# Three PSUM pairs and a bank for the second half of an attention phase: row maxima reduced two at a time

## The chip, the cores and the metric

The kernel runs on one core of one Trainium2 chip. The metric is device time in microseconds of one execution; the time given is the median of three runs. The work is spread over the core's engines: PE (matrix products into PSUM), DVE (VectorE, here above all the row maxima), ACT (ScalarE, here above all the exponentials), POOL, and SP, which issues most DMAs. [...]

## The reference, cut to what matters

```python
h = _layernorm(x) * (1 + ca) + sa
q, k, v = split(h @ wqkv)                 # 16 heads of 28, 2048 tokens
scores = einsum("bhqd,bhkd->bhqk", q, k) * 28 ** -0.5
p = softmax(scores)
o = einsum("bhqk,bhkd->bhqd", p, v)
x = x + ga * (o @ wo)
h = _layernorm(x) * (1 + cb) + sb
x = x + gb * (gelu(_layernorm(h) @ w1 + b1) @ w2 + b2)
```

All inputs are float32. The softmax subtracts the true maximum of each row, so each maximum has to be known before the exponentials of that row are taken.

## The kernel before, in words

There are three stages. First, LayerNorm and the projections. Second, attention. Third, the MLP. The change touches the second stage alone.

The 16 heads go in four groups of four (`g`), the 2048 queries in four tiles of 512 (`qt`); a **unit** `u` is one group and one query tile, 16 units in all. A unit has 16 **steps** (`kt`), each for 128 keys, so there are 256 steps, numbered `step = 16 u + kt`. Each of the four heads of a group takes 32 rows of the PE array, and a matmul of one head uses only those rows, so matmuls of different heads can run side by side.

One step issues, in this order:

- *First scores and second scores* (L1051). The scores of heads 0 and 1 of the group are six matmuls (three terms of a split product, two heads), into a tile `s` of two banks; those of heads 2 and 3 are six more into a second tile `s`. ACT takes the exponential of each tile whole (L1059, 128 x 1024).
- *Maxima* (L392, L397). The scores of later units are computed once more, roughly (one term instead of three), only for their row maxima: one matmul of 32 rows into a bank `mx`, and one VectorE reduction of 128 x 512 to 128 x 1. A unit needs 64 of them. `emit_max` puts three of them into one step and four into the next (`n_maxima`), between the score matmuls, and picks the heads whose rows the scores of that moment leave free.
- *Product with v* (L1015). Four matmuls that use the columns of the array, with the exponentials of the step before, into the bank `o`.

When the last maximum of a unit is in, `max_fin` gathers them, and two steps later their negatives go by DMA into the query operand of that unit.

From unit 12 on, each step with `kt` 8 to 11 also does a 128-token tile of the output projection (`t_wo`, whose matmuls are in `mm_acc`, L317): 9 matmuls in unit 12, 12 in units 13 to 15, of 128 rows and 128 columns, after the product with v, into a bank `mx`. ACT copies the result out (L812) and POOL adds it to `acc` (L813). Call these the **projection steps**; the other steps are plain. With `n_maxima`, a projection step has few maxima or none.

The PSUM banks of this stage: two pairs for `s`, three single banks `mx`, one `o`. When all maxima are done, `share(1, 3)` makes that three pairs `s`, one `mx`, one `o`. A tile waits for the engine that reads the one which had its banks before. A pool hands its tiles out in turn, and the order of instructions on each engine is the order of the code.

Of the kernel before, what the change touches and what calls it, by code (L numbers as in the profile page):

```python
# [22 lines left out]
D = 448  # L23
# [5 lines left out]
NB = S // 512  # L29
NG = H // 4  # L30
NKT = S // 128
# [10 lines left out]
def tile_adaln_block(ctx: ExitStack, tc: tile.TileContext, x, wqkv, wo, w1, b1, w2, b2, c, w_mod, out):  # L42
# [13 lines left out]
    def nm(t):  # L56
        uid[0] += 1
        return f"{t}_{uid[0]}"
# [253 lines left out]
    kh_sb = {}  # L312
    qh_sb = {}

    def mm_acc(p, terms):
        for i, (a, b) in enumerate(terms):
            pe.matmul(p, a, b, start=(i == 0), stop=(i == len(terms) - 1))  # L317

# [173 lines left out]
    def emit_max(n, half=None):  # L492
        for _ in range(n):
# [5 lines left out]
            max_one(g, qt, cch, i, j)  # L499
            count(g, qt, [cch])  # L500


    def emit_task(n, sixth, n_pairs):
        if not n:
# [254 lines left out]
    def unit_end_tasks(u, o_sb):  # L759
        g, qt = divmod(u, NB)  # L760
        st = {}
        staged = g < last_g(qt)
        parts = [g] if g > last_g(qt) else list(range(g + 1))

        def t_den():
            den = sbt("den", [128, 16], bufs=2)
            pool.dma_start(den, o_sb[DH:128:32, :].rearrange("j (q r) -> j q r", r=16))  # L767
            st["den"] = den

        def t_rec():  # L770
# [12 lines left out]
        def t_split2():  # L783
            on = st["on"]
            if u < NU - 1:
                hi = sbt("hi", [128, 512], F32R, bufs=3)
                lo = sbt("lo", [128, 512], F32R, bufs=3)
            else:
                hi = sb.tile([128, 512], F32R, tag=YTAGS[7], name="o_hi", bufs=1)
                lo = sbt("osb", [128, 512], F32R, bufs=2)  # L790
            dve.tensor_copy(hi, on)
            pool.tensor_tensor(out=lo, in0=on, in1=f(hi), op=ALU.subtract)
            st["hi"], st["lo"] = hi, lo
            if staged:
# [193 lines left out]
    pend = None  # L988
    o = None
    plain = [0]  # L990
    three = False


    def is_wo(s_):
        return s_ // NKT >= NU - NB and 8 <= s_ % NKT < 12


    def left_steps(s_):
        rest = range(s_, NKT * (NU - 1) - 6)
        n_wo = sum(is_wo(x) for x in rest)  # L1000
        return len(rest) - n_wo, sum(is_wo(x) and x % NKT > 8 for x in rest)


    def n_maxima(s_):
        n_plain, n_wo = left_steps(s_)
        over = len(mxq) - 7 * n_plain // 2
        if is_wo(s_):
            return max(0, -(-over // max(n_wo, 1))) if s_ % NKT > 8 else 0
        plain[0] += 1
        return 4 if plain[0] % 2 or (over > 3 * n_wo and over > 0) else 3  # L1010

    def av(u, kt, p, o):
        g = u // NB
# [10 lines left out]
        return slot(("c0", "c1", "d0")[p_no[0] % 3], [128, 4, 512], F32)  # L1024

    p_next = p_tile()
    done_max = set()
    for u in range(NU):
        g, qt = divmod(u, NB)
        for kt in range(NKT):  # L1030
            step = u * NKT + kt
            if kt == 1 and u + 1 < NU and u + 1 not in qst:
                load_q(u + 1)
            if kt == NKT - 6 and u + 1 < NU:
# [6 lines left out]
            n = n_maxima(step)  # L1041
            n0 = 1 if n == 3 and step % 4 == 3 else 2

            ks, qs = kst[(g, kt // 4)], qst[u]
            kc = slice((kt % 4) * 128, (kt % 4 + 1) * 128)
            for hf in range(2):
                s2 = ps_s2()
                for term, (kp, qp) in enumerate(((0, 0), (1, 0), (0, 1))):
                    for jj in range(2):
                        rows_ = slice(64 * hf + 32 * jj, 64 * hf + 32 * jj + 32)  # L1050
                        pe.matmul(s2[:, jj, :], ks[rows_, kp, kc], qs[rows_, qp, :], start=(term == 0), stop=(term == 2))  # L1051
                    if hf == 0 and term < min(n0, n):
                        emit_max(1, 1)
                    if hf == 1 and ((term == 0 and n - n0 > 0) or (term == 2 and n - n0 > 1)):
                        emit_max(1, 0)
                if hf == 1:
                    p_next = p_tile()
                    pt.append(p_next[:, 0:2, :])
                act.activation(pt[hf], s2, AF.Exp, scale=SCALE)  # L1059
            if pend is not None:  # L1060
                pu, pkt, pp, po = pend
                av(pu, pkt, pp, po)
# [99 lines left out]
```

## Time and profile before

| what | value |
|---|---|
| median of three runs | 1141.04 us (1140.98 to 1141.12) |
| the profiled execution | 1142.17 us, of which the profile's span covers 1140.4 us |
| PE busy | 1127.8 us, 99% of the span |
| VectorE busy | 831.6 us, 73% |
| ScalarE busy | 683.4 us, 60% |
| granted TensorE clock | 0.998 |
| step 91 | its first exponential begins at 407.3 us |
| steps 200, 216, 232 (the first projection steps of units 12, 13, 14) | their first exponentials begin at 673.8, 721.2, 770.6 us |
| last maximum in the order | step 233 |

How to read it: a busy share is a mean over stages with different limits, and matmuls are pipelined, so PE counts as busy while a matmul is on its way although the next one waits. In attention the length of one step, and what a step waits for, says more. Times in the timeline rows count from the start of the span.

### The profile page before, as it was taken

Reading aid. Unit: us, or ns where it says so; the run is one execution under the profiler, and the core shown is the slowest. Engines: PE = TensorE matmul, PEld = TensorE weight load, DVE = VectorE, ACT = ScalarE, POOL = GpSimd, SP = SyncE. Lnnn points to the kernel's source line nnn. Section 1 sums busy time; section 2 is a strip of 40 time slices with the busy share of each in tenths; the row PEclk is TensorE's granted clock in tenths of the full one; section 3 lists DMA queues with packets and bytes.
Section 4 is the critical chain, followed back from the end, with each engine's and each line's share of the span. In section 5 each row is a group of like instructions: output and inputs, shape, how many; then the busy total and the mean of one; then the engine's idle time right before and its main releaser. Section 6 shows DMA issues by size and latency. Waiting matters only on the chain.

```text
span 1140.4 us, 20798 instructions
## 1 busy us (share of the span) xinstructions
PE 1127.8 (99%) x8380; PEld 678.4 (59%) x8380; DVE 831.6 (73%) x1487; ACT 683.4 (60%) x839; POOL 245.9 (22%) x277
## 2 busy tenths in 40 slices
PE   8999999999999999999999999999999999999998
PEld 6767765444444444444444444545468888888887
DVE  6868787999999999999999977493648853444322
ACT  4655757878878887888788877586762321211110
POOL 2634431211011011101110121214514503123000
PEclk9999999999999999999999999999999999999999
DMA  9543345121222111222211212022113100000000
GB/s 299 194 144 125 111 160 156 38 62 44 67 84 75 53 45 39 76 76 66 66 30 58 89 63 76 10 85 85 53 55 87 43 34 1 1 33 1 33 1 33
DMA packets 50296, 81.12 MB, mean 71 GB/s; under 512 B 12308, under 2 KB 21592, under 8 KB 50200
## 3 DMA queue, kind: packets, MB, share of 16 engines
q1 hardware_dynamic: 44536, 74.83, 20.8%
q0 software_dynamic: 5376, 4.51, 1.5%
q8 instruction: 66, 1.08, 0.4%
q10 hardware_dynamic: 288, 0.46, 0.1%
q14 instruction: 30, 0.25, 0.1%
HBM read 53.11 MB, written 26.35 MB: 70 GB/s over the span
## 4 chain that ended last, share of the span: by engine, by line
PE 95%; DVE 1%; ACT 1%; DMA 1%; issue 1%; POOL 0%; DVEq 0%; ACTq 0%; POOLq 0%
PE s L1051 27%; PE o L1015 22%; PE mx L317 16%; PE pa L339 7%; PE mx L392 7%; PE s L1112 4%; PE s L1113 4%; PE s L1111 4%; PE pa L317 3%; DMA slot_c<-in_w_mod_dram 1%; PE o L240 1%; PE mx L240 1%; PE o L547 0%; ACT slot_c L1059 0%; DMA acc<-in_A_x_dram 0%
## 5 line engine op out<-in xcount | busy, mean ns | idle before, releaser
L397 DVE TENSOR_REDUCE mxp<-mx 128x1 f32<-128x512 f32 x919 | 580.3, 684 | 102.0 <-PE mx L392 95.2
L1059 ACT ACTIVATE slot_c<-s 128x1024 f32<-128x1024 f32 x341 | 339.5, 1022 | 77.1 <-PE s L1051 76.7
L1051 PE MATMUL s<-slot_b,slot_a 32*128 32x512 f32 x3072 | 376.0, 420 | 1.6 <-ACT full L812 0.7
L1051 PEld LDWEIGHTS s<-slot_b,slot_a 32*128 32x128 f32 x3072 | 211.9, 183 | 250.2 <-ACT slot_c L1059 147.9
L392 PE MATMUL mx<-kh,qh 32*128 32x512 f32 x899 | 290.1, 469 | 0.3
L1015 PE MATMUL o<-slot_c,v 128*32 128x512 f32 x1364 | 270.5, 605 | 0.5 <-ACT osb L983 0.4
L1059 ACT ACTIVATE slot_d<-s 128x1024 f32<-128x1024 f32 x171 | 174.7, 1022 | 38.4 <-PE s L1051 38.1
L1015 PE MATMUL o<-slot_d,v 128*32 128x512 f32 x684 | 179.9, 605 | 0.0
L1095 ACT ACTIVATE full<-mx,b_col 128x512 f32<-128x512 f32 x56 | 38.5, 688 | 192.2 <-PE mx L317 180.1
L392 PEld LDWEIGHTS mx<-kh,qh 32*128 32x128 f32 x899 | 115.3, 182 | 7.5 <-DVE mxp L397 1.9
L1098 DVE CAST hi<-full 128x512 fp32r<-128x512 f32 x56 | 25.2, 450 | 129.3 <-ACT full L1095 129.3
L1015 PEld LDWEIGHTS o<-slot_c,v 128*32 128x32 f32 x1364 | 38.0, 108 | 54.9 <-issue 50.1
L317 PE MATMUL mx<-y,slot_a 128*128 128x512 f32 x160 | 60.6, 395 | 0.0
L767 POOL DMA_DIRECT2D den<-osb x16 | 11.4, 716 | 192.5 <-ACT osb L983 192.5
L405 ACT ACTIVATE slot_d<-mx 128x512 f32<-128x512 f32 x48 | 27.0, 597 | 40.0 <-PE mx L392 39.8
L1099 DVE TENSOR_TENSOR lo<-full,hi 128x512 fp32r<-128x512 f32 x56 | 44.1, 788 | 5.6 <-PE mx L240 0.5
L317 PE MATMUL mx<-y,slot_c 128*128 128x512 f32 x152 | 47.5, 396 | 0.1
L1113 PE MATMUL s<-slot_v,lo 128*128 128x448 f32 x128 | 46.7, 365 | 0.0
L1111 PE MATMUL s<-slot_v,hi 128*128 128x448 f32 x128 | 46.6, 364 | 0.0
L1015 PEld LDWEIGHTS o<-slot_d,v 128*32 128x32 f32 x684 | 24.6, 108 | 27.3 <-issue 25.1
L774 POOL DMA_DIRECT2D drec<-den x16 | 9.3, 578 | 145.1 <-DVE den L772 145.1
L317 PE MATMUL mx<-y,slot_v 128*128 128x512 f32 x112 | 39.2, 396 | 0.0
(223 smaller groups left out, 1484.3 us busy)
## 6 DMA issues: line engine op xcount, KB each, us to landing
d<-lo SPq DMA_DIRECT2D x32, 256.0 KB
slot_b<-d SPq DMA_DIRECT2D x32, 256.0 KB
slot_a<-d SPq DMA_DIRECT2D x32, 256.0 KB
d<-hi SPq DMA_DIRECT2D x20, 256.0 KB
osb<-drec POOLq DMA_DIRECT2D x16, 256.0 KB, 5.2
out_dram<-xn SPq DMA_DIRECT2D x16, 224.0 KB
slot_v<-in_w_mod_dram SPq DMA_DIRECT2D x4, 784.0 KB
raw<-in_B_w_dram SPq DMA_DIRECT2D x14, 224.0 KB
```

What stands on the lines that cost most here:

```text
L317: pe.matmul(p, a, b, start=(i == 0), stop=(i == len(terms) - 1))
L339: pe.matmul(p, *ts[i], start=(i == 0), stop=(i == len(ts) - 1))
L392: pe.matmul(m, qh_sb[(g, qt)][js, i * 128 : (i + 1) * 128], k[js, :], start=True, stop=True)
L397: dve.tensor_reduce(out=mxp[(g, qt)][:, i, j, cch : cch + 1], in_=m, op=ALU.max, axis=AX.X)
L1015: pe.matmul(o[32 * j : 32 * j + 32, :], v_sb[kt // 4][:, kt % 4, 4 * g + j, :], p[j // 2][:, j % 2, :], start=(kt == 0), stop=(kt == NKT - 1),
L1051: pe.matmul(s2[:, jj, :], ks[rows_, kp, kc], qs[rows_, qp, :], start=(term == 0), stop=(term == 2))
L1059: act.activation(pt[hf], s2, AF.Exp, scale=SCALE)
L1095: act.activation(gf, p, AF.Gelu_apprx_tanh, bias=b1_col[:, i : i + 1])
L1099: dve.tensor_tensor(out=glo, in0=gf, in1=f(ghi), op=ALU.subtract)
L1111: pe.matmul(pp, ghi[:, ts], w_hi, start=(m == 0), stop=False)
L1112: pe.matmul(pp, ghi[:, ts], w_lo, start=False, stop=False)
L1113: pe.matmul(pp, glo[:, ts], w_hi, start=False, stop=(m == NFT - 1))
```

## The change

From the first step at which three maxima in a plain step and eight in a projection step are enough for every later unit (`room`; that is step 91), PSUM is laid out anew: three pairs `pair0` to `pair2`, one single bank `mx`, one `o`. Up to step 90 everything is as before.

In a plain step the first scores take one pair (always the same one), and then comes one maximum into `mx`. The second scores take another pair, and then come two maxima into the third pair, one into each of its banks. These two have neighbouring heads, and one VectorE operation reduces both (128 x 2 out of 128 x 2 x 512). In the next step the second scores take the pair that held the two maxima, and the maxima take the pair that held the second scores. In odd steps the heads 2 and 3 come first, so that the two maxima always use the rows which the second scores leave free. So each plain step has three maxima instead of three and four by turns.

In a projection step while maxima are left, the result of the projection takes a bank of the first pair, and five maxima (`spare`) are issued between the fifth and the sixth of its matmuls: two pairs and a single one. With the three of the step itself that is eight. The three pairs then change places.

Once the maxima are used up, the three pairs serve the scores by turns. Units are now finished four steps ahead instead of six.

```diff
+    def ps_pair(i):
+        return psp[0].tile([128, 2, 512], F32, tag=f"pair{i}", name=nm("pair"), bufs=1)
...
-    def mm_acc(p, terms):
-        for i, (a, b) in enumerate(terms):
-            pe.matmul(p, a, b, start=(i == 0), stop=(i == len(terms) - 1))
+    def mm_acc(p, terms, done=0, mid=None):
+        for i in range(done, len(terms)):
+            if i == 5 and mid:
+                mid()
+            pe.matmul(p, *terms[i], start=(i == 0), stop=(i == len(terms) - 1))
...
+    def take(half):
+        fits = [x for x, m in enumerate(mxq[:32]) if m[4] // 2 == half]
+        alone = [x for x in fits if mxq[x][:4] + (mxq[x][4] ^ 1,) not in mxq]
+        return mxq.pop((alone or fits or [0])[0])
+
+    def emit_two(half, t):
+        for x, m in enumerate(mxq[:32]):
+            if m[4] == 2 * half and m[:4] + (m[4] + 1,) in mxq[:40]:
+                g, qt, cch, i, j = m
+                mxq.remove(m)
+                mxq.remove(m[:4] + (j + 1,))
+                for y in range(2):
+                    max_mm(g, qt, i, j + y, kh_sb[(g, cch)], lambda: t[:, y, :])
+                dve.tensor_reduce(out=mxp[(g, qt)][:, i, j : j + 2, cch], in_=t, op=ALU.max, axis=AX.X)
+                count(g, qt, [cch, cch])
+                return
+        two = [take(half) for _ in range(min(2, len(mxq)))]
...
+    def emit_one(half):
+        if mxq:
+            m = take(half)
+            max_one(*m)
+            count(*m[:2], [m[2]])
...
-                p = ps_mx()
+                p, spare = wo_banks()
...
-                mm_acc(p[:, :D], terms)
+                mm_acc(p[:, :D], terms, 0, spare)
...
+    def wo_banks():
+        if not mxq:
+            return ps_mx(), None
+        first, g_, b_ = pairs
+        t = ps_pair(first)
+        pairs[:] = [g_, b_, first]
+
+        def spare():
+            for x, i in enumerate((g_, b_)):
+                if mxq:
+                    emit_two(x, ps_pair(i))
+            emit_one(0)
+
+        return t[:, 0, :], spare
...
-            if not (three or mxq or late):
-                three = True
-                share(1, 3)
+            if not pairs and room(step):
+                pairs = [0, 1, 2]
+                share(1, 0)
...
-            for hf in range(2):
-                s2 = ps_s2()
+            halves = (1, 0) if pairs and step % 2 else (0, 1)
+            for x, hf in enumerate(halves):
+                s2 = ps_pair(pairs[x]) if pairs else ps_s2()
...
+                if pairs and x == 0 and not (step and is_wo(step - 1)):
+                    emit_one(halves[1])
...
-                act.activation(pt[hf], s2, AF.Exp, scale=SCALE)
+                act.activation(pt[x], s2, AF.Exp, scale=SCALE)
+            if mxq and pairs:
+                emit_two(halves[0], ps_pair(pairs[2]))
+                if step and is_wo(step - 1):
+                    emit_one(halves[1])
+                pairs = [pairs[0], pairs[2], pairs[1]]
+            elif pairs:
+                pairs = [pairs[2], pairs[0], pairs[1]]
+            pt = [pt[halves[0]], pt[halves[1]]]
```

How the instructions stand now. First, PE in a plain step with four maxima a little after step 91, before: `s` are the scores of the step, `mx` the maxima (from `kh`, `qh`), `o` the product with v; what an instruction waits for is in brackets.

```order
L1051 MATMUL s_1199_5285<-slot_b1_1001_4373,slot_a3_988_4328 128x512 [waits Activation_49]
L1051 MATMUL s_1199_5285<-slot_b1_1001_4373,slot_a3_988_4328 128x512
L392 MATMUL mx_1200_5288<-kh1_1062_4654,qh0_791_3411 128x512 [waits DVE_49]
L1051 MATMUL s_1199_5285<-slot_b1_1001_4373,slot_a3_988_4328 128x512 x2
L392 MATMUL mx_1201_5293<-kh2_1096_4814,qh0_791_3411 128x512 [waits DVE_49]
L1051 MATMUL s_1199_5285<-slot_b1_1001_4373,slot_a3_988_4328 128x512 x2
L1051 MATMUL s_1202_5299<-slot_b1_1001_4373,slot_a3_988_4328 128x512 [waits Activation_49]
L1051 MATMUL s_1202_5299<-slot_b1_1001_4373,slot_a3_988_4328 128x512
L392 MATMUL mx_1203_5302<-kh2_1096_4814,qh0_791_3411 128x512 [waits DVE_49]
L1051 MATMUL s_1202_5299<-slot_b1_1001_4373,slot_a3_988_4328 128x512 x4
L392 MATMUL mx_1204_5309<-kh2_1096_4814,qh0_791_3411 128x512 [waits DVE_49]
L1015 MATMUL o_1116_4908<-slot_d0_1190_5243,v2_257 32x512 x2
```

Both kinds of scores wait for ACT, and the fourth maximum stands behind all six of the second scores. Now the same engine after the change, one whole step; `pair` is a tile of two banks, and the line numbers are those of the changed file (L1095 the scores, L397 the maxima, L1058 the product with v):

```order
L1095 MATMUL pair_1204_5315<-slot_b1_1001_4373,slot_a3_988_4328 128x512 [waits Activation_49]
L1095 MATMUL pair_1204_5315<-slot_b1_1001_4373,slot_a3_988_4328 128x512 x5
L397 MATMUL mx_1205_5322<-kh2_1096_4814,qh0_791_3411 128x512 [waits DVE_49]
L1095 MATMUL pair_1206_5326<-slot_b1_1001_4373,slot_a3_988_4328 128x512 [waits DVE_49]
L1095 MATMUL pair_1206_5326<-slot_b1_1001_4373,slot_a3_988_4328 128x512 x5
L397 MATMUL pair_1208_5335<-kh2_1096_4814,qh0_791_3411 128x512 [waits Activation_49]
L397 MATMUL pair_1208_5335<-kh2_1096_4814,qh0_791_3411 128x512
L1058 MATMUL o_1116_4908<-slot_c0_1197_5277,v3_258 32x512 x2
L1058 MATMUL o_1116_4908<-slot_c1_1202_5305,v3_258 32x512 x2
```

The first scores still wait for ACT; the second scores now wait for DVE, and the pair of maxima behind them for ACT.

Second, PE in a projection step of unit 12, after the change, from its product with v on (L322 is the projection; before, these nine stand together, without maxima between them, and the scores behind them wait for ACT):

```order
L1058 MATMUL o_1785_8333<-slot_c1_1832_8569,v2_257 32x512 x2
L322 MATMUL pair_1844_8631<-slot_e0_514_2139,slot_a2h_1793_8367 128x448 [waits Activation_49]
...
L322 MATMUL pair_1844_8631<-slot_e1_515_2140,slot_a3h_1794_8370 128x448
L397 MATMUL pair_1845_8637<-kh3_1635_7551,qh1_1383_6246 128x512 [waits DVE_49]
L397 MATMUL pair_1845_8637<-kh3_1635_7551,qh1_1383_6246 128x512
L397 MATMUL pair_1846_8641<-kh3_1635_7551,qh1_1383_6246 128x512 [waits Activation_49]
L397 MATMUL pair_1846_8641<-kh3_1635_7551,qh1_1383_6246 128x512
L397 MATMUL mx_1847_8645<-kh3_1635_7551,qh1_1383_6246 128x512 [waits DVE_49]
L322 MATMUL pair_1844_8631<-slot_e0_514_2139,slot_a3h_1794_8370 128x448
...
L1095 MATMUL pair_1849_8655<-slot_b0_1691_7844,slot_a2_1755_8178 128x512 [waits DVE_49]
L1095 MATMUL pair_1849_8655<-slot_b0_1691_7844,slot_a2_1755_8178 128x512 x5
L1095 MATMUL pair_1850_8663<-slot_b0_1691_7844,slot_a2_1755_8178 128x512 [waits DVE_49]
```

Five maxima stand between the fifth and the sixth matmul of the projection, and both halves of the next step's scores wait for DVE.

Third, DVE at the same place after the change, from the step's own pair of maxima on (L521 reduces a pair, L402 a single one):

```order
L521 TENSOR_REDUCE mxp_1757_8188<-pair_1833_8571 128x2 [waits PE_49]
L521 TENSOR_REDUCE mxp_1757_8188<-pair_1835_8585 128x2 [waits PE_49]
L521 TENSOR_REDUCE mxp_1757_8188<-pair_1836_8589 128x2 [waits PE_49]
L402 TENSOR_REDUCE mxp_1757_8188<-mx_1837_8593 128x1 [waits PE_49]
L521 TENSOR_REDUCE mxp_1757_8188<-pair_1842_8620 128x2 [waits PE_49]
L402 TENSOR_REDUCE mxp_1757_8188<-mx_1843_8624 128x1 [waits PE_49]
```

Three pair reductions and two single ones belong to each projection step with eight maxima. In the whole program 928 reductions of one maximum each become 599 of one from single banks, 162 of two, and 5 of one from a pair's bank.

More of the change, by code (lines that the diff above doesn't have):

```diff
@@ L500, in emit_max @@
             count(g, qt, [cch])
+    def take(half):
[14 more added lines that the diff above has]
+        two = [take(half) for _ in range(min(2, len(mxq)))]
+        for y, (g, qt, cch, i, j) in enumerate(two):
+            max_mm(g, qt, i, j, kh_sb[(g, cch)], lambda: t[:, y, :])
+        for y, (g, qt, cch, i, j) in enumerate(two):
+            dve.tensor_reduce(out=mxp[(g, qt)][:, i, j, cch : cch + 1], in_=t[:, y, :], op=ALU.max, axis=AX.X)
+            count(g, qt, [cch])
+    def emit_one(half):
[3 more added lines that the diff above has]
+            count(*m[:2], [m[2]])
     def emit_task(n, sixth, n_pairs):
@@ L990, in tile_adaln_block, with room, finish_step @@
     plain = [0]
-    three = False
+    pairs = []
     def is_wo(s_):
         return s_ // NKT >= NU - NB and 8 <= s_ % NKT < 12
[L998 to L1010, printed above, removed]
+    def room(s_):
+        need = 0
+        for u in range(s_ // NKT, NU):
+            need += left.get(divmod(u, NB), 64)
+            if need > sum(8 if is_wo(x) else 3 for x in range(s_, finish_step(u))):
+                return False
+        return True
+    def finish_step(u):
+        return NKT * u - 4
+    def wo_banks():
[10 more added lines that the diff above has]
+        return t[:, 0, :], spare
     def av(u, kt, p, o):
@@ L1026, in tile_adaln_block @@
     p_next = p_tile()
-    done_max = set()
     for u in range(NU):
@@ L1033, in tile_adaln_block @@
                 load_q(u + 1)
-            if kt == NKT - 6 and u + 1 < NU:
+            if u + 1 < NU and step == finish_step(u + 1):
                 finish_max(*divmod(u + 1, NB))
             tick_late()
-            if not (three or mxq or late):
-                three = True
-                share(1, 3)
+            if not pairs and room(step):
+                pairs = [0, 1, 2]
+                share(1, 0)
             pt = [p_next[:, 2:4, :]]
-            n = n_maxima(step)
+            plain[0] += 1
+            n = 4 if plain[0] % 2 else 3
             n0 = 1 if n == 3 and step % 4 == 3 else 2
@@ L1051, in tile_adaln_block @@
                         pe.matmul(s2[:, jj, :], ks[rows_, kp, kc], qs[rows_, qp, :], start=(term == 0), stop=(term == 2))
-                    if hf == 0 and term < min(n0, n):
+                    if not pairs and hf == 0 and term < min(n0, n):
                         emit_max(1, 1)
-                    if hf == 1 and ((term == 0 and n - n0 > 0) or (term == 2 and n - n0 > 1)):
+                    if not pairs and hf == 1 and ((term == 0 and n - n0 > 0) or (term == 2 and n - n0 > 1)):
                         emit_max(1, 0)
-                if hf == 1:
+                if pairs and x == 0 and not (step and is_wo(step - 1)):
+                    emit_one(halves[1])
+                if x == 1:
                     p_next = p_tile()
                     pt.append(p_next[:, 0:2, :])
-                act.activation(pt[hf], s2, AF.Exp, scale=SCALE)
+                act.activation(pt[x], s2, AF.Exp, scale=SCALE)
[7 more added lines that the diff above has]
+            pt = [pt[halves[0]], pt[halves[1]]]
             if pend is not None:
```

## The prediction

> **What bounds the kernel now.** I read the page first, then a table of the stretches between steps, then the timeline of two plain steps, then the waits. From the page, the busy shares and the row of slices for VectorE:
>
> ```profile
> PE 1127.8 (99%) x8380; PEld 678.4 (59%) x8380; DVE 831.6 (73%) x1487; ACT 683.4 (60%) x839; POOL 245.9 (22%) x277
> DVE  6868787999999999999999977493648853444322
> ```
>
> VectorE stands at 9 through most of attention, and PE at 99% of the span, so both look like the bound. Steps decide it. I cut the time from step 91 to step 236 at the first exponentials. The columns are the stretch, its length, and the busy time (with instructions) of PE, weight loads, DVE, ACT and POOL, then the granted clock, DMA share and GB/s.
>
> ```profile
> 406.99:673.84 266.85, 266.85 (x2566) 118.15 (x2560) 244.39 (x408) 215.35 (x225) 32.53 (x42) 1.00 0.22 64
> 673.84:691.53 17.69, 17.69 (x132) 10.57 (x134) 6.15 (x10) 9.89 (x12) 4.75 (x5) 1.00 0.00 1
> 691.53:720.90 29.37, 29.37 (x278) 12.76 (x275) 26.45 (x45) 23.70 (x25) 4.03 (x6) 1.00 0.26 83
> 720.90:740.90 20.00, 20.00 (x145) 12.58 (x142) 5.15 (x9) 10.01 (x13) 5.04 (x6) 1.00 0.00 1
> 740.90:770.40 29.50, 29.50 (x280) 12.97 (x278) 26.32 (x44) 23.75 (x25) 4.35 (x5) 1.00 0.25 82
> 770.40:790.40 20.00, 19.32 (x138) 12.06 (x136) 5.89 (x16) 9.96 (x13) 5.76 (x6) 1.00 0.07 15
> ```
>
> Row one is the 109 plain steps 91 to 199, 2.448 us each. Then come four projection steps of unit 12 (4.42 each), twelve plain ones, four of unit 13 (5.00), twelve plain, four of unit 14 (5.00). VectorE is busy for 92% of row one, yet it is not full, and in the projection steps it is busy for a quarter to a third. Two plain steps in the timeline (start, length, engine, line; the idle time before is in brackets):
>
> ```profile
> 450.31 0.49 PE L1051 MATMUL s<-slot_b,slot_a 32*128 32x512 f32 x2
> 450.31 0.51 PE L392 MATMUL mx<-kh,qh 32*128 32x512 f32 x2
> 450.64 0.65 PE L1051 MATMUL s<-slot_b,slot_a 32*128 32x512 f32 x8
> ...
> 451.11 0.39 PE L392 MATMUL mx<-kh,qh 32*128 32x512 f32 x1
> ...
> 451.32 1.02 ACT L1059 ACTIVATE slot_d<-s 128x1024 f32<-128x1024 f32 x1 [0.81 <-PE s L1051]
> ...
> 451.46 0.62 PE L1015 MATMUL o<-slot_c,v 128*32 128x512 f32 x2
> ...
> 452.24 1.02 ACT L1059 ACTIVATE slot_c<-s 128x1024 f32<-128x1024 f32 x1
> ...
> 452.45 0.50 PE L1051 MATMUL s<-slot_b,slot_a 32*128 32x512 f32 x2
> ...
> 452.46 0.50 PE L392 MATMUL mx<-kh,qh 32*128 32x512 f32 x2
> ...
> 453.02 2.48 DVE L397 TENSOR_REDUCE mxp<-mx 128x1 f32<-128x512 f32 x4 [0.25 <-PE mx L392]
> 453.31 0.18 PEld L1051 LDWEIGHTS s<-slot_b,slot_a 32*128 32x128 f32 x2 [0.33 <-ACT slot_c L1059]
> ...
> 453.46 1.94 ACT L1059 ACTIVATE slot_c<-s 128x1024 f32<-128x1024 f32 x2 [0.20 <-PE s L1051]
> ...
> 453.77 0.49 PE L392 MATMUL mx<-kh,qh 32*128 32x512 f32 x1
> 453.88 0.40 PE L1051 MATMUL s<-slot_b,slot_a 32*128 32x512 f32 x2
> 454.20 0.62 PE L1015 MATMUL o<-slot_d,v 128*32 128x512 f32 x2
> ...
> 455.20 0.50 PE L1051 MATMUL s<-slot_b,slot_a 32*128 32x512 f32 x2
> ```
>
> The two steps take 2.14 and 2.75. In the first, all four row groups work at once: four rounds of matmuls at 450.31, 450.64, 450.88 (inside the row of eight) and 451.11, then the product with v at 451.46. In the second, the second scores wait until 453.31 for ACT, since their pair still holds the scores of the step before: ACT's exponential from 452.24 ends at 453.26. This makes a loop. Call S the time from a step's first scores to the next step's: first scores at 450.31, their exponential 1.01 later (451.32), the second exponential 0.92 after that, its end 1.02 later, the release 0.05 later: 3.00 in all until the second scores of the *next* step. From there 0.89 to the product with v (454.20), and 1.00 more to the next first scores (455.20): 1.89. Two steps cost 3.00 + 1.89 = 4.89, one 2.45, and row one says 2.448. So plain steps are bound by two pairs for the scores, through ACT's latency, and not by VectorE's throughput. The waits say the same: the largest of PE are of the weight loads of the scores for the exponentials.
>
> ```profile
> PEld s L1051 <- ACT slot_c L1059: 147.9, 223, 0.8
> PEld s L1051 <- ACT slot_d L1059: 74.8, 113, 0.8
> ```
>
> **The change part by part.** *Plain steps.* What is new is that the second scores go into the pair which held the maxima, so they wait for VectorE's reduction of the step before, no longer for the exponential. The reduction of two maxima is not in the trace; I size it by its nearest rows (line, shapes, count, busy, mean ns):
>
> ```profile
> L397 DVE TENSOR_REDUCE mxp<-mx 128x1 f32<-128x512 f32 x919 | 580.3, 684 | 102.0 <-PE mx L392 95.2 <-PE s L1051 4.5
> L429 DVE TENSOR_REDUCE m<-mxp 128x16 fp32r<-128x64 f32 x13 | 2.9, 220 | 0.4
> ```
>
> From 64 to 512 elements it grows by 464 ns, 1.04 ns per element, so 1024 elements cost 684 + 530 = 1.21 us. The floor is 1.04 x 1024 = 1.06 with no fixed part; the ceiling two reductions in a row, 0.60 + 0.68 = 1.28 (0.60 is their spacing in the row of four at 453.02). I take 1.21, since both rows are the same operation.
>
> The new loop: the pair of maxima takes the fourth round of its rows, 0.80 after the first scores (451.11 against 450.31). It needs the exponential of the previous step's second scores, free at 3.00 - S; with S about 2.2 that is 0.80 too, so neither waits much. Its reduction starts 0.07 after the matmul's end (452.46 + 0.50 to 453.02 is 0.06), so at 0.80 + 0.39 + 0.07 = 1.26. It ends at 2.47, and the release makes 2.52: then the second scores of the next step may start. With 1.89 behind it, two steps are 4.41 and one is **2.21**. The other limits lie below: four rounds without a wait 2.14, two exponentials 1.94, VectorE 0.60 + 1.13 = 1.73. The single maximum waits for nothing: its bank is free 1.26 after its own matmul's step began. Three maxima where 3.5 stood take nothing from PE, since they ran in rows that were free.
>
> 109 steps at 2.448 - 2.21 save 266.85 - 240.9 = 26.0 us, the 24 plain steps between the projections 58.87 - 53.0 = 5.8. Together **-31.8**.
>
> *Projection steps.* Half a maximum less in each of 133 plain steps makes 66 that land here, eight maxima per step. Rows of PE in step 200, from the product with v on:
>
> ```profile
> 674.59 0.62 PE L1015 MATMUL o<-slot_d,v 128*32 128x512 f32 x2
> ...
> 675.59 0.88 PE L317 MATMUL mx<-slot_e,slot_a2h 128*128 128x448 f32 x3
> 676.30 0.78 PE L317 MATMUL mx<-slot_e,slot_a3h 128*128 128x448 f32 x3
> 676.91 0.57 PE L317 MATMUL mx<-slot_e,hi 128*128 128x448 f32 x2
> 677.32 0.37 PE L317 MATMUL mx<-slot_e,lo 128*128 128x448 f32 x1
> 677.62 0.50 PE L1051 MATMUL s<-slot_b,slot_a 32*128 32x512 f32 x2
> ```
>
> The fifth projection matmul starts 0.91 after the first, and a change to row groups costs 0.30 from the last one (677.32 to 677.62). So, from the projection's start: maxima at 1.22; first pair reduced from 1.78 (0.56 after a first matmul, as at 453.02) to 2.99; second pair, spaced by 1.13, until 4.12; the single one until 4.72. The first scores of the next step take the first of these pairs: at 3.04. The second scores take the second: at 4.17. With 0.89 and 1.00 behind it the next projection starts at **6.06**, where 4.42 and 5.00 stand now, and VectorE, which had nothing to do there, is the chain. Nothing covers this: PE waits at the second scores, and the exponentials, the product with v and the projection are queued behind them. From the first scores of 200 to those of 204: 2.21 + 3.04 + 3 x 6.06 = 23.4 against 17.69, so +5.7, and step 204, which still has its second scores behind the last reductions, takes 6.06 - 3.04 = 3.02, +0.8. Unit 13 has twelve matmuls. The single maximum takes a second round at 1.55, 0.35 later (as from 451.11 to 451.46) the sixth matmul starts, at 1.90, the seventh 0.31 behind it and the rest 0.20 apart, so the last at 3.23 and the first scores at 3.53 by PE itself: 23.9 against 20.00, +3.9, and +0.3 for step 220. Unit 14 has eight maxima in steps 232 and 233, four in 234 (one of them inside the projection) and none in 235: about 22.3 against 20.00, +2.3. Together **+13.0**.
>
> *Smaller ones.* ACT copies `o` at each unit's end:
>
> ```profile
> L983 ACT COPY osb<-o 128x512 f32<-128x512 f32 x16 | 9.4, 588 | 1.2 <-PE o L1015 1.2
> ```
>
> These 0.59 were covered by ACT's pause of half a microsecond per step (2.45 - 1.94). The pause falls to 2.21 - 1.94 = 0.27, so I charge 0.25 for eight ends: +2; without any cover it would be 4.7. The division's DMA chain runs by steps; with shorter ones VectorE waits for it a little longer before projections, and now the second scores wait for VectorE: +1. The change of pools at step 91: +0.3. The deadline of four steps instead of six costs nothing: in the order no unit's maxima are complete later than five steps ahead of its first scores, so their negatives leave three steps ahead, some 6.6 us, and their DMAs run beside plain steps. If they come late, the first scores of one unit wait; I put that under the range.
>
> Sum: -31.8 + 13.0 + 3.3 = **-15.5**. The profiled execution of 1142.17 would be 1126.7; it is 1.1 above the median, and 1141.04 - 15.5 gives 1125.5, rounded to **1126**.
>
> **The rivals.** *A. Matmuls start in the order of the program.* Then the single maximum would start with the third round of the first scores (0.57), the second scores behind it, and the pair of maxima with or after their last round (1.04), so that the product with v starts at 1.38 and a step takes 2.38. The plain steps would save 133 x 0.07 = 9, while the projections lose 13 and some 2.5 more for a longer score phase, with 3.3 beside: 1141 + 10 = **1151**. It decides from 0.23 on that the pair of maxima starts later than I have it: each 0.1 is 0.05 on a step, 6.7 in all, against the 15.5. Against it stands 453.77: this maximum stands behind all six second scores in the order, and started before the last two, at 453.88. [...] Chance 0.08.
>
> *B. VectorE is late.* If a pair costs 1.28, or small operations of VectorE (waits for DMA or POOL in its queue) come between, a step is 2.25 to 2.30 and a projection 6.2 to 6.4: +6 to +13, **1132 to 1139**. For it: the loop has no slack at all on VectorE's side, and each 0.1 us of delay there costs half of that. Against: VectorE has 0.4 us per step to spare. Chance 0.15.
>
> *C. No stall at all.* The 1.89 was measured with weight loads that restart after a wait. If they do not, a step takes the 2.14 of four rounds: 133 x 0.07 = 9 less, **1117**. Chance 0.12.
>
> *D. The pairs do not come about*, so that single reductions remain. In the order 162 reductions take two maxima and 5 stand split, so this is as good as excluded. Chance 0.01.
>
> **How the numbers follow.** The forecast 1126 has 0.64 and its own range is 1121 to 1131. The range goes down to C and up to B's end: 1116 to 1139, leaving out A and about a tenth beside. Faster by over 0.2% (2.3 us, about what a measurement tells from no change): forecast, C and nearly all of B, 0.88. The same: 0.03. Slower: A and mishaps not named, 0.09.
>
> **What would show it.** Right: plain steps after 91 of about 2.2 us, with the weight loads of the second scores released by the reduction of a pair; pair reductions of about 1.21; projection steps of about 6 with VectorE busy for nearly all of a projection run, where it is now busy for a third; nothing changed ahead of step 91 and behind step 236. Wrong: steps of 2.4 with the pair of maxima at 1.0 or later (A), reductions of 1.28 or more or gaps in VectorE's queue (B), steps of 2.14 (C), or first scores that wait for a DMA at a unit's start.

## The result, and the profile after

The changed kernel takes **1153.34 us** (median of four runs, 1152.60 to 1154.12) against 1141.08 for the kernel before on the same chip: ratio 1.0106, interval 1.0088 to 1.0123. It is slower by 12.3 us, where 15 less was forecast. The profiled execution has a span of 1152.2 us at a granted clock of 0.999.

The same two parts of the page, busy shares and the slices of VectorE:

```profile
PE 1137.9 (99%) x8380; PEld 685.8 (60%) x8380; DVE 822.3 (71%) x1325; ACT 682.9 (59%) x839; POOL 245.7 (21%) x277
DVE  6868787999999977777777777776738863444322
```

VectorE has 162 instructions less and stands at 7 where it stood at 9. It did become freer; the plain steps hardly became shorter. The stretches between the first exponentials of steps 91, 200, 204, 216, 220, 232 and 236 (columns as before):

```profile
407.69:670.52 262.83, 262.83 (x2508) 119.66 (x2507) 204.39 (x243) 214.65 (x226) 31.59 (x41) 1.00 0.22 65
670.52:694.81 24.29, 23.45 (x145) 11.88 (x141) 18.43 (x19) 10.21 (x13) 4.97 (x6) 1.00 0.00 1
694.81:725.02 30.21, 30.09 (x283) 13.99 (x285) 23.47 (x30) 23.80 (x25) 4.18 (x6) 1.00 0.24 80
725.02:749.72 24.70, 24.70 (x161) 14.43 (x157) 18.85 (x21) 9.89 (x13) 4.83 (x6) 1.00 0.00 1
749.72:779.51 29.79, 29.79 (x283) 13.67 (x279) 22.96 (x28) 23.70 (x26) 4.16 (x5) 1.00 0.26 82
779.51:802.51 23.00, 23.00 (x155) 13.66 (x153) 16.70 (x29) 9.89 (x13) 5.99 (x7) 1.00 0.06 13
```

The rows of before that the prediction shows were cut up to 0.3 us ahead of some of these exponentials; cut at them exactly, the kernel before has 266.54, 17.69, 29.63, 19.91, 29.55 and 20.02, from 407.31 to 790.65. So the 109 plain steps of row one take 2.411 us each instead of 2.445, -3.7 in all. The projection stretches cost +6.60, +4.79 and +2.98, together +14.4. The plain steps between them take 0.8 more, and row one starts 0.4 later. At the last mark the changed kernel is 802.51 - 790.65 = 11.9 us behind, which is the whole difference of the spans (11.8).

So the projection steps cost what was forecast and a little more, and the plain steps gave almost nothing. One plain step in the timeline:

```profile
505.50 0.50 PE L1095 MATMUL pair<-slot_b,slot_a 32*128 32x512 f32 x2
...
505.52 0.49 PE L397 MATMUL mx<-kh,qh 32*128 32x512 f32 x1
...
505.83 0.71 PE L1095 MATMUL pair<-slot_b,slot_a 32*128 32x512 f32 x6
...
506.30 0.39 PE L397 MATMUL pair<-kh,qh 32*128 32x512 f32 x2
506.37 0.64 PE L1095 MATMUL pair<-slot_b,slot_a 32*128 32x512 f32 x4
506.50 1.03 ACT L1105 ACTIVATE slot_c<-pair 128x1024 f32<-128x1024 f32 x1 [0.44 <-PE pair L1095]
506.54 0.69 DVE L402 TENSOR_REDUCE mxp<-mx 128x1 f32<-128x512 f32 x1 [0.55 <-PE pair L1095]
...
507.15 1.22 DVE L521 TENSOR_REDUCE mxp<-pair 128x2 f32<-128x1024 f32 x1
...
507.94 0.50 PE L1095 MATMUL pair<-slot_b,slot_a 32*128 32x512 f32 x2
```

The pair of maxima starts at 506.30, 0.80 after the first scores, just as forecast. Its reduction starts only at 507.15, 1.65 after them, not 1.26. VectorE was busy with the *single* maximum, and that is the row to look at. Its matmul starts at 505.52, with the first round of the first scores, and ends at 506.01. Its reduction starts at 506.54: half a microsecond during which VectorE is idle, and the bracket names as releaser not the matmul `mx` but the scores into `pair`. In the order of the program this maximum stands behind all six matmuls of the first scores, and ACT's exponential of those six starts at 506.50, 0.04 ahead of the reduction. So VectorE got the maximum when ACT got the scores, and not when the maximum's own record ended. From the start of the pair's reduction the rest goes as forecast: 507.15 + 1.22 + 0.05 makes 508.42, where the second scores of the next step start (508.418 in the single records), and (2.92 + 1.89) / 2 = 2.405.

The groups of the two reductions in the changed kernel (count, busy and mean ns, then the idle time ahead and its releasers) say the same over the whole run:

```profile
L402 DVE TENSOR_REDUCE mxp<-mx 128x1 f32<-128x512 f32 x590 | 382.1, 685 | 116.0 <-PE pair L1095 70.4 <-PE mx L397 43.9 <-PE pair L397 0.5
...
L521 DVE TENSOR_REDUCE mxp<-pair 128x2 f32<-128x1024 f32 x162 | 196.4, 1217 | 13.6 <-PE pair L397 9.0 <-PE pair L1095 4.1
```

In the kernel before, 95.2 of the 102.0 us of idle time ahead of such a reduction ended with its own matmul; here 70.4 of 116.0 end with the scores. The second row is the new reduction of a pair, 1217 ns.

### The profile page after: what moved, and what is told of

Same layout as the page of the kernel before. It is cut to its first block, busy times and chain, and to the rows that moved or that the text cites. A ratio compares the mean times of both kernels' runs of the same rounds, so it can differ in the third digit from the quotient of the medians.

```text
span 1152.2 us, 20638 instructions
## 1 busy us (share of the span) xinstructions
PE 1137.9 (99%) x8380; PEld 685.8 (60%) x8380; DVE 822.3 (71%) x1325; ACT 682.9 (59%) x839; POOL 245.7 (21%) x277
## 4 chain that ended last, share of the span: by engine, by line
PE 94%; DVE 2%; ACT 1%; DMA 1%; issue 1%; POOL 0%; DVEq 0%; ACTq 0%; POOLq 0%
PE o L1058 22%; PE pair L1095 17%; PE mx L322 13%; PE s L1095 10%; PE pa L344 7%; PE mx L397 5%; PE s L1166 4%; PE s L1167 4%; PE s L1165 4%; PE pa L322 3%; PE pair L397 2%; PE pair L322 2%; DVE mxp L521 1%; DMA slot_c<-in_w_mod_dram 1%; PE o L243 1%
## 5 line engine op out<-in xcount | busy, mean ns | idle before, releaser
L402 DVE TENSOR_REDUCE mxp<-mx 128x1 f32<-128x512 f32 x590 | 382.1, 685 | 116.0 <-PE pair L1095 70.4
L1058 PE MATMUL o<-slot_c,v 128*32 128x512 f32 x1364 | 270.5, 605 | 0.4 <-ACT osb L1017 0.4
L1105 ACT ACTIVATE slot_c<-pair 128x1024 f32<-128x1024 f32 x220 | 219.1, 1022 | 45.6 <-PE pair L1095 45.1
L1095 PE MATMUL pair<-slot_b,slot_a 32*128 32x512 f32 x1980 | 238.6, 425 | 1.3 <-DVE mxp L521 0.7
L1095 PEld LDWEIGHTS pair<-slot_b,slot_a 32*128 32x128 f32 x1980 | 147.2, 183 | 147.3 <-ACT slot_c L1105 73.8
L521 DVE TENSOR_REDUCE mxp<-pair 128x2 f32<-128x1024 f32 x162 | 196.4, 1217 | 13.6 <-PE pair L397 9.0
L397 PE MATMUL mx<-kh,qh 32*128 32x512 f32 x570 | 202.7, 472 | 0.3
L1058 PE MATMUL o<-slot_d,v 128*32 128x512 f32 x684 | 179.9, 605 | 1.0 <-ACT slot_d L1105 1.0
L1095 PE MATMUL s<-slot_b,slot_a 32*128 32x512 f32 x1092 | 138.0, 420 | 0.9 <-ACT v L381 0.6
L1105 ACT ACTIVATE slot_c<-s 128x1024 f32<-128x1024 f32 x121 | 120.5, 1022 | 30.2 <-PE s L1095 30.2
L1095 PEld LDWEIGHTS s<-slot_b,slot_a 32*128 32x128 f32 x1092 | 77.8, 183 | 94.4 <-ACT slot_c L1105 59.1
L1105 ACT ACTIVATE slot_d<-pair 128x1024 f32<-128x1024 f32 x110 | 112.4, 1022 | 24.1 <-PE pair L1095 23.6
L397 PEld LDWEIGHTS mx<-kh,qh 32*128 32x128 f32 x570 | 79.2, 182 | 5.5 <-DVE mxp L402 1.8
L1058 PEld LDWEIGHTS o<-slot_c,v 128*32 128x32 f32 x1364 | 38.0, 108 | 59.3 <-issue 52.9
L1105 ACT ACTIVATE slot_d<-s 128x1024 f32<-128x1024 f32 x61 | 62.3, 1022 | 14.0 <-PE s L1095 13.9
L397 PE MATMUL pair<-kh,qh 32*128 32x512 f32 x329 | 63.8, 408 | 0.0
L322 PE MATMUL mx<-y,slot_a 128*128 128x512 f32 x160 | 60.6, 395 | 0.0
```

What stands on the lines that cost most here:

```text
L322: pe.matmul(p, *terms[i], start=(i == 0), stop=(i == len(terms) - 1))
L397: pe.matmul(m, qh_sb[(g, qt)][js, i * 128 : (i + 1) * 128], k[js, :], start=True, stop=True)
L402: dve.tensor_reduce(out=mxp[(g, qt)][:, i, j, cch : cch + 1], in_=m, op=ALU.max, axis=AX.X)
L521: dve.tensor_reduce(out=mxp[(g, qt)][:, i, j : j + 2, cch], in_=t, op=ALU.max, axis=AX.X)
L1058: pe.matmul(o[32 * j : 32 * j + 32, :], v_sb[kt // 4][:, kt % 4, 4 * g + j, :], p[j // 2][:, j % 2, :], start=(kt == 0), stop=(kt == NKT - 1),
L1105: act.activation(pt[x], s2, AF.Exp, scale=SCALE)
```

## The experiments

The theory: a matmul of other rows may start ahead of its turn (505.52), but the engine that waits for its result starts only when the matmuls ahead of it in the program are done (506.54). I call this **signals in order**. Its rivals: matmuls *start* in order (rival A of the prediction), or VectorE is late for a reason of its own (B). Whether the maximum's own result comes late, or VectorE's wait takes in the matmuls ahead of it as well, was not shown: by both the reduction starts behind them.

### The single maximum alone is moved ahead

```diff
+    if pairs and x == 0 and term == 0 and not (step and is_wo(step - 1)):
+        emit_one(halves[1])
...
-if pairs and x == 0 and not (step and is_wo(step - 1)):
-    emit_one(halves[1])
```

It now stands behind the first term of the first scores, so behind two matmuls instead of six.

> The single maximum of a plain step is issued behind the first term of the first scores (two matmuls) and no longer behind all six; all else as in the changed kernel. Signal theory (matmuls of other row groups run early, but a matmul's end is told in the order of the program, so VectorE sees the single maximum only when the six scores ahead of it are done): its reduction starts about 0.57 us after the first scores and not 1.04; the pair's reduction then starts when the second scores ahead of it are done, s + 1.03 (s: when the second scores start), so a plain step is 2.30 instead of 2.405, and the time 1153 - 133 x 0.105 = 1139. VectorE theory (its work of 1.73 us per step plus small operations cannot be done sooner, or it reads PSUM late for a reason of its own): no change, 1153. Theory of starts in program order: the maximum starts earlier by two rounds, and the second scores with it, so about 2.2 and 1126.

Measured: 1143.51 us (1141.66 to 1144.81), ratio 1.0011, interval 1.0002 to 1.0020. The stretch from step 91 to step 200, in the columns of the stretches:

```profile
405.95:659.77 253.82, 253.82 (x2508) 117.88 (x2507) 213.23 (x244) 214.10 (x225) 31.64 (x41) 1.00 0.23 67
```

A step in its timeline:

```profile
507.26 0.50 PE L1095 MATMUL pair<-slot_b,slot_a 32*128 32x512 f32 x2
...
507.26 0.50 PE L397 MATMUL mx<-kh,qh 32*128 32x512 f32 x1
...
507.83 0.69 DVE L402 TENSOR_REDUCE mxp<-mx 128x1 f32<-128x512 f32 x1 [0.19 <-PE mx L397]
...
508.74 1.23 DVE L521 TENSOR_REDUCE mxp<-pair 128x2 f32<-128x1024 f32 x1 [0.22 <-PE pair L1095]
```

The single maximum's matmul starts when it did, with the first round, but its reduction now follows at 0.57 instead of 1.04. Ten us come back. Plain steps are 2.329, not the 2.30 I expected: VectorE is free at 508.52 and yet waits 0.22 for the pair, until 1.48 after the first scores. The pair stands behind all six second scores, and the bracket of its reduction names the scores (508.74), so it is late too.

### The pair of maxima alone is moved ahead

```diff
+    if pairs and x == 1 and term == 1:
+        more = bool(mxq)
+        if more:
+            emit_two(halves[0], ps_pair(pairs[2]))
...
-if mxq and pairs:
-    emit_two(halves[0], ps_pair(pairs[2]))
```

The pair now stands behind the second of the three terms of the second scores.

> Only the pair of maxima is issued earlier (behind the second term of the second scores); the single one stays behind all six of the first scores. Signal theory: the single one is still told at 1.04, VectorE is busy with it until 1.65, and the pair's reduction starts then as now: no change, 1153 (1151 to 1154). VectorE theory: no change either. Theory of starts in program order: the pair starts a round earlier, 0.1 less per step, 1140.

Measured: 1151.81 us (1151.09 to 1152.45), ratio 1.0089, interval 1.0074 to 1.0104; the plain stretch is 262.35 against 262.83. As long as VectorE is held by the late single maximum, an earlier pair is worth nothing. This speaks against a wait that belongs to the pair's place alone, and against starts in program order, by which 1140 was expected. It does not separate signals in order from a VectorE that is late for a reason of its own: by both the time stays.

### Both are moved ahead

The two edits together.

> As the run with the single maximum early, and in addition the pair of maxima is issued behind the second of the three terms of the second scores. Signal theory: the pair's end is told behind two of the three rounds of the second scores, reduction from 1.26 as the prediction had it, plain step 2.21 to 2.22, time 1153 - 133 x 0.19 = 1128. VectorE theory: 1153.

Measured: 1132.82 us (1131.74 to 1133.63), ratio 0.9925, interval 0.9909 to 0.9942: faster than the kernel before, and 5 us above the 1128 expected. The stretches from step 91 to 200 and from 200 to 204:

```profile
406.93:651.98 245.05, 245.05 (x2510) 105.27 (x2507) 212.56 (x244) 214.19 (x226) 31.57 (x41) 1.00 0.24 70
651.98:676.17 24.19, 23.30 (x145) 11.86 (x143) 18.21 (x19) 10.22 (x13) 5.01 (x6) 1.00 0.00 1
```

A step in its timeline, from the last exponential of the step before:

```profile
504.75 1.02 ACT L1109 ACTIVATE slot_c<-pair 128x1024 f32<-128x1024 f32 x1
...
505.11 0.50 PE L1095 MATMUL pair<-slot_b,slot_a 32*128 32x512 f32 x2
...
505.68 0.69 DVE L402 TENSOR_REDUCE mxp<-mx 128x1 f32<-128x512 f32 x1 [0.39 <-PE mx L397]
505.82 0.19 PEld L397 LDWEIGHTS pair<-kh,qh 32*128 32x128 f32 x2 [0.17 <-ACT slot_c L1109]
...
506.36 1.23 DVE L521 TENSOR_REDUCE mxp<-pair 128x2 f32<-128x1024 f32 x1
```

Now the pair's reduction starts at 1.25, the value of the prediction, and plain steps take 2.248. That is 0.04 above the loop's (1.25 + 1.22 + 0.05 + 1.89) / 2 = 2.205. At 505.82 the weights of the pair of maxima wait for ACT, whose exponential of the step before ends at 505.77; that is the third pair's own loop, which the prediction had put at "neither waits much". I take it for the missing 0.04, which on 133 steps would be those 5 us, but no run separates it.

### A dose: the single maximum behind the second term

The layout of the last run, with one place changed.

```diff
-    if pairs and x == 0 and term == 0 and not (step and is_wo(step - 1)):
+    if pairs and x == 0 and term == 1 and not (step and is_wo(step - 1)):
```

> A dose: both maxima early, but the single maximum behind the second term of the first scores (four matmuls ahead of it in the program) instead of the first (two) or the third (six). Signals in order: its reduction starts at about 0.81 after the first scores, between 0.573 (two ahead) and 1.04 (six ahead), although its matmul starts with the first round in all three; VectorE then takes the pair at 0.81 + 0.61 = 1.42 instead of 1.255, and a plain step grows by half of 0.16: 2.245 + 0.08 at most; since the run with the pair at 1.486 had 2.33, I expect 2.29, and 1138 against 1132.8. If a signal came with the matmul's own end, the single's reduction stays at 0.573 and the time at 1133. If a maximum must stand ahead of all but the first round to be early at all, 1.04 again and 1145 or more.

Measured: 1138.45 us (1136.04 to 1139.50), ratio 0.9966, interval 0.9955 to 0.9977. The stretch from step 91 to 200:

```profile
408.89:658.96 250.07, 250.07 (x2508) 113.42 (x2507) 204.30 (x244) 214.57 (x226) 31.51 (x41) 1.00 0.23 68
```

A step in its timeline:

```profile
506.61 0.50 PE L1095 MATMUL pair<-slot_b,slot_a 32*128 32x512 f32 x2
...
506.62 0.50 PE L397 MATMUL mx<-kh,qh 32*128 32x512 f32 x1
...
507.42 0.69 DVE L402 TENSOR_REDUCE mxp<-mx 128x1 f32<-128x512 f32 x1 [0.17 <-PE pair L1095]
...
508.02 1.22 DVE L521 TENSOR_REDUCE mxp<-pair 128x2 f32<-128x1024 f32 x1
```

The matmul starts with the first round (506.62 against 506.61), as in every such row above; its reduction follows at 0.81. With two, four and six matmuls ahead of it in the program the reduction starts at 0.57, 0.81 and 1.04: one round of scores each, which took 0.24 and 0.23 in the prediction's first plain step (450.64, 450.88, 451.11). Plain steps follow the start of the pair's reduction through the loop, with nothing else adjusted:

| kernel | pair's reduction after the first scores | loop, worked out | plain step, measured |
|---|---|---|---|
| both early | 1.25 | 2.205 | 2.248 |
| single behind the second term | 1.41 | 2.285 | 2.294 |
| single early, pair late | 1.48 | 2.32 | 2.329 |
| changed kernel | 1.65 | 2.405 | 2.411 |

### The same in the old layout

The kernel before, with only the maxima of the first half moved:

```diff
-if hf == 0 and term < min(n0, n):
-    emit_max(1, 1)
+if hf == 0 and term == 2:
+    emit_max(min(n0, n), 1)
```

> The old layout (four banks of scores, three of maxima, one reduction per maximum) with one edit: the one or two maxima that stand between the terms of the first scores stand behind all six of them. Signals in order: the first reduction of a step moves from 0.57 to 1.04 after its first scores, while the matmul itself still starts with the first round where its bank is free. Since this layout is bound by the loop through ACT, and VectorE is busy for 92%, the time grows by less than in the new layout: 0 to 0.1 per plain step of the 200, 1141 to 1160, I take 1148. If a signal came with the matmul's own end, reductions stay at 0.57 and the time at 1141.

Measured: 1194.15 us (1193.26 to 1194.39), ratio 1.0455, interval 1.0432 to 1.0477. The stretch from step 91 to 200:

```profile
429.19:720.64 291.45, 291.21 (x2557) 122.17 (x2556) 243.31 (x408) 215.62 (x226) 31.98 (x41) 1.00 0.20 59
```

A step of four maxima in its timeline:

```profile
478.47 0.50 PE L1051 MATMUL s<-slot_b,slot_a 32*128 32x512 f32 x2
...
478.49 0.72 PE L392 MATMUL mx<-kh,qh 32*128 32x512 f32 x2
...
479.51 2.49 DVE L397 TENSOR_REDUCE mxp<-mx 128x1 f32<-128x512 f32 x4 [0.25 <-PE s L1051]
...
480.26 0.18 PEld L392 LDWEIGHTS mx<-kh,qh 32*128 32x128 f32 x1 [0.41 <-DVE mxp L397]
480.26 0.50 PE L392 MATMUL mx<-kh,qh 32*128 32x512 f32 x1
```

The first reduction starts at 1.04 here too, though its matmul started with the first round (478.49). So the late reduction is no matter of the new layout. My size was far off: 2.674 per plain step instead of at most 2.55. I had counted VectorE's share and forgotten the banks. With three of them, the fourth maximum of a step waits for the first reduction (480.26), and the product with v stands behind it. The whole lateness, 0.47, arrives in every second step (3.21 instead of 2.74).

### Six maxima in a projection step

Both early, and `spare` with one pair and a single one instead of two pairs and a single one:

```diff
-            for x, i in enumerate((g_, b_)):
-                if mxq:
-                    emit_two(x, ps_pair(i))
+            if mxq:
+                emit_two(1, ps_pair(b_))
...
-            if need > sum(8 if is_wo(x) else 3 for x in range(s_, finish_step(u))):
+            if need > sum(6 if is_wo(x) else 3 for x in range(s_, finish_step(u))):
```

> Both maxima early as before, and a projection step has six maxima instead of eight: inside the projection one pair (in the pair that the second scores of the next step take) and one single. Fewer maxima there mean that the new layout starts at step 115 and not 91. Theory that the projection steps are a chain of reductions: the first scores behind a projection no longer wait for VectorE; unit 12's projection steps 4.9 instead of 6.29, unit 13's 5.3. Sum against the kernel before: 109 plain steps x 0.23 = -25, projections +4.6, rest +3: 1141 - 18 = 1123. If projection steps are long for another reason (the change of the array's mode twice more per step), they stay near 6 and the time is 1135.

Measured: 1131.19 us (1129.82 to 1132.04), ratio 0.9908, interval 0.9893 to 0.9922. The new layout can then begin only at step 115. The expectation of 1123 counted the gain on all 109 plain steps all the same; steps 91 to 199 took 250.49 against 266.54 before, 16 less and not 25. Unit 12 takes 20.41 for its four projection steps instead of 24.19, 5.1 each instead of 6.0 on average: the price of a projection step is set by the maxima in it. But unit 13 took 24.28, since the last of its four steps took 7.48. The timeline of VectorE in that step:

```profile
725.54 0.68 DVE L402 TENSOR_REDUCE mxp<-mx 128x1 f32<-128x512 f32 x1
726.81 0.69 DVE L402 TENSOR_REDUCE mxp<-mx 128x1 f32<-128x512 f32 x1 [0.59 <-PE mx L397]
728.09 0.69 DVE L402 TENSOR_REDUCE mxp<-mx 128x1 f32<-128x512 f32 x1 [0.59 <-PE mx L397]
```

Three single maxima go one after the other through one bank, some 1.28 apart. Two of them are what `finish_max` found left at the deadline, four steps ahead of unit 14.

### The same with a margin

```diff
-            if need > sum(6 if is_wo(x) else 3 for x in range(s_, finish_step(u))):
+            if need and need + 4 > sum(6 if is_wo(x) else 3 for x in range(s_, finish_step(u))):
```

> Six maxima per projection step, as in the run before, but the pairs start only when four places are to spare (step 123 instead of 115). In the run before, the last steps ahead of unit 14 had too few places, so two maxima were worked off one after the other at a deadline, and one projection step took 7.48 instead of 5.65. If that deadline is the cause, this step takes 5.65 again and the steps behind it 2.9 and 2.35; eight more steps stay at 2.446 instead of 2.245, +1.6, and the sum is -2.9 + 1.6: about 1130. If the long step comes from something else (a DMA, the division's chain), it stays, and the time is 1133.

Measured: **1129.59 us** (1128.29 to 1130.95), ratio 0.9892, interval 0.9871 to 0.9912. The three projection stretches:

```profile
657.03:677.47 20.44, 20.44 (x145) 11.50 (x144) 14.90 (x19) 9.89 (x13) 5.00 (x6) 1.00 0.00 1
705.09:727.45 22.36, 22.36 (x157) 12.96 (x152) 14.62 (x17) 9.89 (x13) 4.98 (x6) 1.00 0.00 1
755.05:777.27 22.22, 22.22 (x155) 13.12 (x157) 16.86 (x30) 9.89 (x12) 6.88 (x8) 1.00 0.01 1
```

The long step is gone (22.36 instead of 24.28), so the deadline was its cause. Against the run without a margin the intervals overlap, so that the gain of 1.6 is not shown by the times, only by that stretch. Against both the kernel before and the changed one this version is faster.

## Why the prediction was wrong

**The step that failed: "The single maximum waits for nothing"**, and with it the start of the pair's reduction at 1.26. The matmul indeed waits for nothing, but the reduction of it does. The prediction took the delay from a matmul's start to its reduction (0.56 at 453.02) from a maximum with two matmuls ahead of it, and applied it to one with six. It had the single maximum's bank free after 1.26; it came free after 1.73 (506.54 + 0.69 - 505.50). The row at 453.77, used against rival A, showed a *start* ahead of turn and was read as if the result came ahead too. Rival B's "0.4 us per step to spare" counted how much VectorE has to do, not when it may begin. VectorE was late by 507.15 - 505.50 - 1.26 = 0.39; half of it on each of 133 plain steps is 26, which leaves 6 of the gain of 31.8. Measured were -3.7 for the 109 steps and +0.8 for the stretches between, -2.9 in all. In the stretches between, the two steps behind each projection run (3.41 and 2.77, then 2.96 and 2.78 between first exponentials) are 2.3 above four steps of 2.41; the prediction had +1.1 for them.

**The loop was right.** That two steps cost the time up to the next second scores plus 1.89 holds to 0.01 in three kernels of the table and to 0.04 in the fourth, the run with both early. Half of a delay on VectorE's side arrives in a step, as rival B's sentence had it: from the run with the single behind the second term to the changed kernel the pair's reduction is 0.24 later and a step 0.117 longer.

**The reduction of a pair was right**: 1217 ns measured, 1.21 forecast. Rival B's reason, a dearer pair, was not the case; nor did small operations come between (the pair's reduction at 507.15 follows the single one's at 506.54 at once). VectorE was late, but because it had idled before.

**The projection steps: mechanism right, size short.** Four steps were put at 23.4, 23.9 and about 22.3, and measured 24.29, 24.70 and 23.00. One period in the timeline of the changed kernel:

```profile
688.63 0.50 PE L1095 MATMUL pair<-slot_b,slot_a 32*128 32x512 f32 x2 [0.17 <-DVE mxp L521]
...
689.44 0.39 PE L397 MATMUL mx<-kh,qh 32*128 32x512 f32 x1
...
689.76 0.11 PEld L1058 LDWEIGHTS o<-slot_d,v 128*32 128x32 f32 x2 [0.34 <-issue]
...
690.75 0.51 PEld L322 LDWEIGHTS pair<-slot_e,slot_a2h 128*128 128x128 f32 x3 [0.84 <-ACT slot_c L1105]
...
692.52 2.36 DVE L521 TENSOR_REDUCE mxp<-pair 128x2 f32<-128x1024 f32 x2 [1.02 <-PE pair L397]
...
693.80 0.96 PE L1095 MATMUL pair<-slot_b,slot_a 32*128 32x512 f32 x6
...
694.93 0.50 PE L1095 MATMUL pair<-slot_b,slot_a 32*128 32x512 f32 x2 [0.17 <-DVE mxp L521]
```

From the projection's start at 690.75: the pairs' reductions at 1.77 (forecast 1.78), first scores at 3.05 (3.04), second scores at 4.18 (4.17). From second scores to the product with v it is 1.13 (688.63 to 689.76), not the 0.89 taken from a plain step: the step's own single maximum takes a round more (689.44), which the product follows. With 0.99 up to the next projection a period is 6.30, not 6.06. That is the term that was mis-sized, 0.24 per period; three periods make 0.7 of the 0.9 and of the 0.8 that units 12 and 13 took beyond the forecast. VectorE was to be busy for nearly all of a projection run; it is busy for 18.43 of 24.29, since in the period shown it idles 1.02 ahead of the first pair that stands inside the projection (692.52) and 0.51 ahead of the step's own pair (689.68).

**The smaller terms.** The change of pools makes the step ahead of row one 0.5 longer (3.23 instead of 2.74; forecast 0.3). The +2 for copies of `o` and +1 for the division's chain were meant for steps of 2.21, which did not come; they cannot be told apart here. Nothing else was lost ahead of step 91, nor behind step 236, as forecast.

**The rivals.** A gave 1151, within 3 us of the result, but its mechanism is not what the rows show, so that its number came near is no evidence for it. The pair of maxima started at 0.80, not 1.04, and the single one with the first round, not the third (505.52). In these rows the order of the program shows in when a reduction starts (506.54), not in when its matmul does. C did not come, and D neither (162 reductions of pairs).

With the two terms put right, the sum of the prediction is -15.5 + 26 + 2.4 = +12.9 (2.4 is what the three projection runs took beyond the forecast), against 12.3 measured; the steps behind the projections and the smaller terms make up the rest, and I did not separate them further.

## What to carry to other kernels

When engines wait for a matmul that shares the array with others, count the matmuls ahead of it in the *program*, not the moment at which its record starts: here the reduction began 0.57, 0.81 and 1.04 us after the first round with two, four and six of them ahead. A result that another engine needs soon was better placed ahead of work that nobody waits for yet. Two moves turned 12 us of loss into 9 of gain, with the same instructions. And when a loop has been found that bounds a step, put each waiting engine's queue into it: a reduction that nobody waits for still delayed the one that everybody waited for, here by 0.39 us.

## What the runs showed of the hardware

A matmul of 32 rows started 0.02 us after the first round although six matmuls stood ahead of it (505.52), and its consumer began 0.57, 0.81 or 1.04 us after that round with two, four or six matmuls ahead, in two different layouts (1.04 in the old one as well). In all 109 plain steps 91 to 199 of the changed kernel the idle time ahead of the single maximum's reduction, 58.5 us together or 0.54 each, ended, by the profile, with a matmul of the scores and not with the maximum's own. The ends of matmuls in the trace are modelled; whether the result lay ready in PSUM all that time was not tried.
